# Local attention in 64 by 64 blocks with the band as a product on VectorE, whole turns of q and k, joined tails, token weights in halves, and a new written order

## The chip, the cores and the metric

The kernel runs on one core of a Trainium2 chip. A core has TensorE (PE, with its weight loads listed apart as PEld), VectorE (DVE), ScalarE (ACT), GpSimd (POOL) and SyncE (SP), which here issues all the DMAs. The metric is the device time of one execution in microseconds (us). The kernel before takes 266.62 us in the median of three runs (266.14 to 268.71).

## The reference

The first half is an attention of 8 batches and 8 heads over 576 tokens of 64 channels, made of two parts that are added. The pooled part takes means over 4 tokens, a full softmax attention over the 144 means, and repeats each result 4 times. The local part is a softmax over the keys that lie less than 4 tokens from the query.

```python
q_d = q.reshape(B, H, Sd, 4, D).mean(axis=3)          # and k_d, v_d
out_up = np.repeat(sm_attn(q_d, k_d, v_d), 4, axis=2)
mask = np.abs(pos[:, None] - pos[None, :]) < 4
scores = np.where(mask, scale * q @ k.T, -1e9)
out_local = softmax(scores) @ v
x = (out_up + out_local)                              # batch, 576, 512
```

The second half works on x, token by channel, with a mix over tokens and one over channels:

```python
theta = x @ w_theta
y = w_tok_r @ (x * cos(theta)) + w_tok_i @ (x * sin(theta))
u = x + y
out = u + np.maximum(u @ w_ch, 0.0)
```

Inputs and output are float32; the kernel's products are taken in bfloat16 and summed in float32.

## The kernel before, in words

The work goes batch by batch through generators, one per stage. A string, `ORDER`, has one letter for each step, and each letter runs one step of its stage's generator; `pin` ties every instruction to the one issued before it on its engine, so the string is the order of every engine's queue, SP's too. Several batches are under way at once, and the string was laid out so that steps of different batches stand between each other.

The letters are: L loads (`load`), C casts to bfloat16 (`cast`), A turns of q, k and pooled v (`turns`), S scores (`scores`), N pooled output (`pooled_out`), V local output (`outputs`), T transposes into x (`transposes`), H the product with w_theta with its cosine and sine (`phases`), Z the product of x with these (`modulate`), X the token mix (`mix`), R the channel mix (`channels`), O the last sum and the store (`store`), and l, c, W and D for the weights' loads, casts and turns and for filler matmuls (`warm_up`).

**Turns.** Batches 0 and 1 (`WIDE`) load q and k as 128 partitions of 9 tokens by 64 channels, a run of 2,304 bytes each, and turn them with small matmuls on 64 rows (L299); VectorE sums fours of tokens. Batches 2 to 7 load 96 tokens at a time in runs of 256 bytes, and one matmul with `ip` (L329), an identity with a pooling matrix beside it, gives the turned block and its sums; ScalarE and VectorE copy these out of PSUM in 12 steps (L332, L334 and L336 to L340).

**Local attention.** The queries are cut into 5 chunks of 120, each with 128 keys. For each chunk 8 matmuls (L426, 64 rows and up to 128 columns of weights, two heads beside each other on the two halves of TensorE's rows) write the scores, one exponential on ScalarE empties them (L434), and two selects on GpSimd clear what is outside the band (L447, L449); in batch 0 a product on VectorE does that instead (L440). Then 8 matmuls (L504) make the output and the sum of each row, and VectorE divides (L511, L513).

**Second half.** `mix` makes 8 groups of 9 matmuls a batch (L610) and adds x on VectorE (L614). The last 64 of the 576 tokens, the tail, go a way of their own: in `channels` they take 8 matmuls with 64 columns of weights (L640), and in `mix` and `store` their own copies, DMA transposes (L619) and stores (L662).

**Buffers.** PSUM has two tiles of two banks (`w2`) and four of one bank (`w1`), each used in rotation. Staged loads have 8 buffers, output tiles (`osb`) 4.

Of the kernel before, what the change touches and what calls it, by code (L numbers as in the profile page):

```python
# [15 lines left out]
P = 128  # L16
# [11 lines left out]
QS = [0, 120, 240, 360, 480]  # L28
QC = [120, 120, 120, 120, 96]
KS = [0, 116, 236, 356, 476]  # L30
KW = [128, 128, 128, 128, 100]
QN = [128, 128, 128, 128, 96]
NCH = 5

WIDE = 2
WR = 9
WP = S // WR
TR = 96
TP = TR // 4
TW = TR + TP  # L40

KP = 32

HALF = 64
OC = [128, 128, 128, 128, 64]
# [3 lines left out]
def kernel(  # L49
# [15 lines left out]
    stg = ctx.enter_context(tc.tile_pool(name="stg", bufs=8))  # L65
# [5 lines left out]

    turn2, turn1 = itertools.cycle("ab"), itertools.cycle("abcd")

    def w2(name):
        return ps2.tile([P, 2, 512], FP32, tag="w2" + next(turn2), name=name)
# [3 lines left out]


    staged = {}
    inputs = {}

    def stage(b, key):
        t = staged[b, key] = stg.tile([P, 1024], FP32, tag="st", name=f"st{b}_{key}")
        return t

    def load(b):

        if b < WIDE:  # L90
            for hh in range(4):
                for nm, src in zip("qk", (q, k)):
                    nc.sync.dma_start(
                        out=stage(b, f"{nm}{hh}")[:, 0:WR * D],
                        in_=src[b, 2 * hh:2 * hh + 2].rearrange("h (p r) d -> (h p) (r d)", r=WR),
                    )
                    yield
        else:
            for nm, src in zip("qk", (q, k)):
                for i in range(3):  # L100
                    t = stage(b, f"{nm}{i}")[0:TR].rearrange("p (c h d) -> p c h d", c=2, d=D)
                    for j in range(2):
                        c = 2 * i + j
                        nc.sync.dma_start(
                            out=t[:, j], in_=src[b, :, TR * c:TR * c + TR, :].rearrange("h p d -> p h d"),
                        )
                    yield
        for i in range(3):
            t = stage(b, f"v{i}").rearrange("p (c h d) -> p c h d", c=2, d=D)
            for c in range(2 * i, min(2 * i + 2, NCH)):  # L110
                nc.sync.dma_start(
                    out=t[0:KW[c], c % 2],
                    in_=v[b, :, KS[c]:KS[c] + KW[c], :].rearrange("h p d -> p h d"),
                )
            yield

    def cast(b):

        dims = [P, 2, WR, 2, D] if b < WIDE else [P, 6, H, D]
        q_tm = work.tile(dims, BF16, tag="q_tm", bufs=1, name=f"q_tm{b}")  # L120
        k_tm = work.tile(dims, BF16, tag="k_tm", bufs=1, name=f"k_tm{b}")
        v_w = v_ws[b % 2]
        inputs[b] = (q_tm, k_tm, v_w)
        eng = CASTS.get(b, CASTS[None])
        if b < WIDE:
            for hh in range(4):
                for i, dst in enumerate((q_tm, k_tm)):
                    eng[i](out=dst[:, hh // 2, :, hh % 2, :],
                           in_=staged.pop((b, f"{'qk'[i]}{hh}"))[:, 0:WR * D].rearrange("p (r d) -> p r d", d=D))
                    yield  # L130
        else:
            for i, dst in enumerate((q_tm, k_tm)):
                for c in range(3):
                    eng[i](out=dst[0:TR, 2 * c:2 * c + 2].rearrange("p c h d -> p (c h d)"),  # L134
                           in_=staged.pop((b, f"{'qk'[i]}{c}"))[0:TR])
                    yield
# [148 lines left out]
    def turns(b):  # L285
# [75 lines left out]
        for s in range(2):  # L361
# [5 lines left out]
            )  # L367
        yield

    pds, pms, xds, tmps = {}, {}, {}, {}  # L370

    def slot(b, h):

# [363 lines left out]
```

## Time and profile before

| | before |
|---|---|
| runs, median (lowest to highest) | 266.62 us (266.14 to 268.71) |
| profiled execution, first to last instruction | 266.2 us |
| PE busy | 239.5 us, 90% |
| VectorE busy | 180.8 us, 68% |
| ScalarE busy | 165.9 us, 62% |
| GpSimd busy | 167.9 us, 63% |
| DMA queue, share of 16 engines | 84.2% |
| DMA packets under 512 bytes | 121,777 of 131,155 |
| ScalarE table loads | 18 of 1,283 ns |

The span of the profiled execution lies 0.4 us under the median of the runs; the profile gives no other time of that execution. Busy time of TensorE is modelled from overlapping matmuls, so the rate of a form is better read from the distance between the starts of rows in the timeline than from the mean duration.

### The profile page before, as it was taken

To read this page: it belongs to the slowest core of one execution; us is meant where nothing else is said; L and a number is where in the kernel's file an instruction comes from. 1 tells how busy PE (TensorE), PEld (TensorE's weight loads), DVE (VectorE), ACT (ScalarE), POOL (GpSimd) and SP (SyncE) were. 2 spreads that over 40 slices of the span, in tenths; PEclk is the share of its full clock that TensorE was granted. 3 is DMA by queue.
4 is the path that set the end of the run, shared out by engine and by line. 5 is a ranking of instruction groups with operands and counts; after the bars stand their busy time and mean duration, and the time that the engine had idled before them with its cause. 6 is when DMAs were issued, how large, how long until landed. Compare 5 with 4: busy or idle time off the path is not lost. (4 is left out here: it accounts for less than half of the span.)

```text
span 266.2 us, 7362 instructions
## 1 busy us (share of the span) xinstructions
PE 239.5 (90%) x2880; PEld 164.6 (62%) x2880; DVE 180.8 (68%) x406; ACT 165.9 (62%) x312; POOL 167.9 (63%) x223
## 2 busy tenths in 40 slices
PE   2467898989988999899999999989999999999990
PEld 1234555778655777577676778756658666777740
DVE  3566998867495656875695767756877658855443
ACT  3663289663997699836987787547865699350000
POOL 4459746997989757686939467968765892400000
PEclk9999999999999999999999999999999999999997
DMA  7998999998989995599857998998779942304446
GB/s 230 314 284 283 317 224 188 208 201 168 222 139 213 236 198 115 117 196 284 176 110 144 243 258 147 111 216 207 184 154 210 270 88 64 102 21 105 105 149 215
DMA packets 131155, 49.34 MB, mean 185 GB/s; under 512 B 121777, under 2 KB 122801, under 8 KB 131121
## 3 DMA queue, kind: packets, MB, share of 16 engines
q1 hardware_dynamic: 131120, 48.88, 84.2%
q8 instruction: 22, 0.36, 0.6%
q14 instruction: 13, 0.10, 0.2%
HBM read 33.65 MB, written 9.44 MB: 162 GB/s over the span
## 5 line engine op out<-in xcount | busy, mean ns | idle before, releaser
L610 PE MATMUL psu<-WT,z 128*128 128x288 bf16 x576 | 79.5, 286 | 0.0
L610 PEld LDWEIGHTS <-z 128*128 128x128 bf16 x576 | 53.8, 98 | 14.7 <-issue 0.4
L434 ACT ACTIVATE pm<-psS 128x1024 bf16<-128x1024 f32 (+1 forms) x40 | 38.6, 989 | 16.7 <-PE psS L426 15.5
L614 DVE TENSOR_TENSOR uT<-psu,xT 128x288 bf16<-128x288 f32 x64 | 28.9, 454 | 28.2 <-PE psu L610 28.0
L447 POOL TENSOR_SCALAR_AFFINE_SELECT pm<-pm 128x1024 bf16<-128x1024 bf16 (+1 forms) x35 | 36.7, 1049 | 14.1 <-ACT pm L434 14.1
L449 POOL TENSOR_SCALAR_AFFINE_SELECT pm<-pm 128x1024 bf16<-128x1024 bf16 (+1 forms) x35 | 36.8, 1051 | 2.4
L553 PE MATMUL psth<-wth,xT 128*128 128x512 bf16 x128 | 32.4, 379 | 0.6 <-DVE xT L535 0.4
L632 PE MATMUL psr<-wch,uT 128*128 128x512 bf16 x128 | 31.4, 379 | 0.6 <-DVE xT L535 0.6
L140 POOL CAST v_w<-st_v 128x1024 bf16<-128x1024 f32 (+1 forms) x24 | 21.9, 916 | 15.2 <-DMA st_v<-in_v_dram 15.2
L332 ACT CAST kT<-pstr 128x384 bf16<-128x384 f32 x36 | 17.6, 489 | 19.0 <-PE pstr L329 18.8
L513 DVE TENSOR_TENSOR tmp<-psloc,rl 120x512 bf16<-120x512 f32 (+1 forms) x40 | 27.6, 690 | 1.4
L558 ACT ACTIVATE cs<-psth,pihc 128x512 bf16<-128x512 f32 x32 | 22.2, 693 | 9.1 <-PE psth L553 5.3
L535 DVE TENSOR_TENSOR xT<-xTps,xdT 128x480 bf16<-128x480 bf16 (+1 forms) x40 | 24.9, 631 | 3.7 <-PE xTps L534 3.6
L654 DVE SCALAR_TENSOR_TENSOR osb<-psr,ur 128x512 f32<-128x512 f32 x32 | 21.5, 684 | 6.4 <-PE psr L632 4.3
L617 POOL COPY ut<-uT 128x64 bf16<-128x64 bf16 x32 | 7.3, 237 | 27.7 <-DVE uT L614 22.6
L134 POOL CAST k_tm<-st_k 96x1024 bf16<-96x1024 f32 x18 | 18.9, 1051 | 7.8 <-DMA st_k<-in_k_dram 5.5
L134 POOL CAST q_tm<-st_q 96x1024 bf16<-96x1024 f32 x18 | 18.8, 1048 | 7.6 <-DMA st_q<-in_q_dram 7.6
L588 DVE TENSOR_TENSOR z<-psxt,cs 128x1024 bf16<-128x1024 bf16 x32 | 21.5, 682 | 3.1 <-PE psxt L587 3.0
L332 ACT CAST qT<-pstr 128x384 bf16<-128x384 f32 x36 | 16.9, 484 | 8.6 <-PE pstr L329 8.5
L334 DVE CAST qdT<-pstr 128x96 bf16<-128x96 f32 x36 | 9.1, 255 | 17.4 <-ACT qT L332 16.9
L559 ACT ACTIVATE cs<-psth 128x512 bf16<-128x512 f32 x32 | 19.2, 600 | 0.0
L632 PEld LDWEIGHTS <-uT 128*128 128x128 bf16 x128 | 11.5, 97 | 11.7 <-DVE xT L535 0.6
(97 smaller groups left out, 419.0 us busy)
## 6 DMA issues: line engine op xcount, KB each, us to landing
st_v<-in_v_dram SPq DMA_DIRECT2D x32, 256.0 KB, 5.0
out_dram<-osb SPq DMA_DIRECT2D x32, 256.0 KB, 3.2
st_q<-in_q_dram SPq DMA_DIRECT2D x36, 192.0 KB, 4.9
st_k<-in_k_dram SPq DMA_DIRECT2D x36, 192.0 KB, 4.1
st_q<-in_q_dram SPq DMA_DIRECT2D x8, 288.0 KB, 4.9
st_k<-in_k_dram SPq DMA_DIRECT2D x8, 288.0 KB, 5.4
st_v<-in_v_dram SPq DMA_DIRECT2D x8, 200.0 KB
stw_tok<-in_moe_w_tok_r_dram SPq DMA_DIRECT2D x4, 288.0 KB
```

The lines of the kernel that those rows point to most:

```text
L134: eng[i](out=dst[0:TR, 2 * c:2 * c + 2].rearrange("p c h d -> p (c h d)"), in_=staged.pop((b, f"{'qk'[i]}{c}"))[0:TR])
L332: nc.scalar.copy(out=To[:, :, TR * c:TR * c + TR], in_=ps[:, :, 0:TR])
L434: nc.scalar.activation(out=pv, in_=ps[0:kw].rearrange("p e (j w) -> p (e j) w", w=P)[:, :, 0:qn], func=AF.Exp, scale=SCL,)
L447: nc.gpsimd.affine_select(out=pv, in_=pv, compare_op=ALU.is_ge, fill=0.0, base=off, pattern=[[0, 8], [-1, qn]], channel_multiplier=1)
L449: nc.gpsimd.affine_select(out=pv, in_=pv, compare_op=ALU.is_ge, fill=0.0, base=6 - off, pattern=[[0, 8], [1, qn]], channel_multiplier=-1)
L513: nc.vector.tensor_tensor(out=tmp[0:cnt].rearrange("p (e j d) -> p e j d", e=2, j=4), in0=pv[0:cnt, :, :, 0:D], in1=rl[0:cnt].unsqueeze(3) ...
L535: nc.vector.tensor_tensor(out=xT[:, :, QS[c]:QS[c] + cnt].rearrange("p e (m j) -> p e m j", j=4), in0=ps[:, :, 0:cnt].rearrange("p e (m j) ...
L553: nc.tensor.matmul(out=th, lhsT=xT[:, dc, P * c:P * c + P], rhs=wth[:, dc, :], start=(dc == 0), stop=(dc == 3),)
L558: nc.scalar.activation(out=cs[:, 0, :], in_=th, func=AF.Sin, bias=pihc, scale=1.0)
L610: nc.tensor.matmul(out=ps[:, 0:288], lhsT=z[:, j, P * dc:P * dc + P], rhs=WT[:, j, cols], start=(j == 0), stop=(j == 8),)
L614: nc.vector.tensor_tensor(out=uT[:, dc, cols], in0=ps[:, 0:288], in1=xT[:, dc, cols], op=ALU.add)
L632: nc.tensor.matmul(out=psr, lhsT=uT[:, dc, P * c:P * c + P], rhs=wch[:, dc, :], start=(dc == 0), stop=(dc == 3),)
```

## The change

All batches now load q and k as 2,304-byte runs, turn them with 9 full transposes of 128 by 128 to a group of four heads (`turns`, 4 steps a batch, each emptied by one ScalarE copy of 1,152 elements), and take the sums of four apart (`sums`): those of k on VectorE, those of q on GpSimd with two additions, but in batch 0 on VectorE. The tokens are cut into 10 blocks of 58, each with a window of 64; queries and keys have the same window. Two blocks make a chunk and lie on the two halves of the partitions, so score and output matmuls work on 64 rows by 64 columns of TensorE's array, four tiles beside each other. Two chunks share one exponential. The band is a product on VectorE in all batches (`masks`). The tails of two batches are joined to 128 rows for their transposes, channel mix and store. Token weights come in two halves of their output tokens, and batch 0 mixes the first half first. Residual transposes, the last sums and the stores are steps of their own. Staged loads have 15 smaller buffers, output tiles 5, and there are 4 filler steps in place of 5, all at the end. `ORDER` is new, with 814 letters for 658.

```diff
...
-WIDE = 2
...
+W = 64
+STEP = 58
+CH = 2 * STEP
+W0 = [min(max(STEP * n - 3, 0), S - W) for n in range(10)]
+OWN = [min(STEP, S - STEP * n) for n in range(10)]
+UNITS = [(0, 1), (2, 3), (4,)]
...
-    stg = ctx.enter_context(tc.tile_pool(name="stg", bufs=8))
+    stg = ctx.enter_context(tc.tile_pool(name="stg", bufs=15))
...
     def load(b):
+        for hh in range(4):
+            for nm, src in (("k", k), ("q", q)):
+                nc.sync.dma_start(out=stage(b, f"{nm}{hh}"),
+                                  in_=src[b, 2 * hh:2 * hh + 2].rearrange("h (p r) d -> (h p) (r d)", r=WR))
+                yield
+        for c in range(NCH):
+            t = stage(b, f"v{c}")[:, 0:DM].rearrange("p (h d) -> p h d", d=D)
+            for g in range(2):
+                lo = W0[2 * c + g]
+                nc.sync.dma_start(out=t[W * g:W * g + W], in_=v[b, :, lo:lo + W, :].rearrange("h p d -> p h d"))
+            yield
...
-    CASTS = {0: (act, gp, gp), None: (gp, gp, gp)}
+    CASTS = {0: (act, dve, gp), None: (gp, gp, gp)}
...
     def turns(b):
+        for i in range(2):
+            for n, (tm, To) in enumerate(((k_tm, kT), (q_tm, qT))):
+                ps = w2(f"pstr{n}{i}_{b}", BF16).rearrange("p k e -> p (k e)")
+                for r in range(WR):
+                    nc.tensor.transpose(out=ps[:, P * r:P * r + P], in_=tm[:, i, r, :, :], identity=ident)
+                EVAC[n](
+                    out=To[:, 2 * i:2 * i + 2, 0:S].rearrange("p a (w r) -> p a w r", r=WR),
+                    in_=ps[:, 0:P * WR].rearrange("p (r a w) -> p a w r", a=2, w=W),
                 )
+                yield
...
+    EVAC = (act, act)
...
+    def sums(b):
+        for i in range(2):
...
+                nc.vector.tensor_reduce(out=kd[:, hs, :, 0:PG].rearrange("p e g m -> p (e g) m"), axis=AX.X, op=ALU.add,
+                                      in_=kT[:, hs, :].rearrange("p e (g m j) -> p (e g) m j", m=PG, j=4))
+                yield
+                if i < QSUM.get(b, QSUM[None]):
+                    nc.vector.tensor_reduce(out=qdT[:, hs, :], axis=AX.X, op=ALU.add,
+                                            in_=qT[:, hs, :].rearrange("p e (m j) -> p e m j", j=4))
                 else:
...
+                    nc.gpsimd.tensor_tensor(out=two, in0=four[:, :, 0:2], in1=four[:, :, 2:4], op=ALU.add)
+                    nc.gpsimd.tensor_tensor(out=qdT[:, hs, :].rearrange("p e m -> p (e m)"),
+                                            in0=two[:, :, 0], in1=two[:, :, 1], op=ALU.add)
+                yield
...
+    QSUM = {0: 2, None: 0}
...
+    def scores(b):
+        for u, cs in enumerate(UNITS):
...
+            ps = w2(f"psS{u}_{b}")
+            for i, c in enumerate(cs):
+                for hh in range(4):
+                    for g in range(2):
+                        lo = W0[2 * c + g]
+                        for e in range(2):
+                            nc.tensor.matmul(
+                                out=ps[W * g:W * g + W, e, 4 * W * i + W * hh:4 * W * i + W * hh + W],
+                                lhsT=kT[64 * e:64 * e + 64, hh, lo:lo + W],
+                                rhs=qT[64 * e:64 * e + 64, hh, lo:lo + W],
+                                start=True, stop=True,
+                            )
+            pm = pms[b, u] = work.tile([P, 2, n, 4, W], BF16, tag=f"pm{n}", bufs=3, name=f"pm{u}_{b}")
+            nc.scalar.activation(out=pm.rearrange("p e c j w -> p e (c j w)"), in_=ps[:, :, 0:4 * W * n],
+                                 func=AF.Exp, scale=SCL)
+            yield
...
+    def masks(b):
+        for u, cs in enumerate(UNITS):
...
+            MASK.tensor_tensor(out=pv, in0=pv, in1=band.unsqueeze(1).to_broadcast([P, n, W]), op=ALU.mult)
+            yield
...
+    MASK = nc.vector
...
     def outputs(b):
+        for u, cs in enumerate(UNITS):
+            for i, c in enumerate(cs):
...
+                for j in range(4):
+                    for hf in range(2):
...
+                        for g in range(2):
+                            nc.tensor.matmul(
+                                out=pv[W * hf:W * hf + W, g, j, :],
+                                lhsT=pms[b, u][W * g:W * g + W, e, i, blk, :],
+                                rhs=v_w[W * g:W * g + W, c, 4 * hf + j, 0:65],
+                                start=(j == 0), stop=(j == 3),
+                            )
...
     def transposes(b):
...
+            for g in range(2):
...
+                for kk in range(2):
+                    nc.tensor.matmul(
+                        out=ps[:, kk::2, STEP * g:STEP * g + OWN[n]],
+                        lhsT=tmp[:, g, P * kk:P * kk + P], rhs=identw[:, :, lo:lo + OWN[n]],
+                        start=True, stop=True,
+                    )
...
+    def tail_channels(i):
+        ut = uts[i]
+        psr = rels["t", i] = w1(f"psrt_{i}")
+        for dc in range(4):
+            nc.tensor.matmul(out=psr, lhsT=ut[:, dc, :, :], rhs=wch[:, dc, :], start=(dc == 0), stop=(dc == 3))
+        yield
...
-            osb = moep.tile([P, DM], FP32, tag="osb", bufs=4, name=f"osb{c}_{b}")
+            osb = osbs[b, c] = moep.tile([P, DM], FP32, tag="osb", bufs=5, name=f"osb{c}_{b}")
...
-    WARM = 5
+    WARM = 4
...
+        P=each(pooled_scores), S=each(scores), M=each(masks), N=each(pooled_out), n=each(pooled_turn),
+        V=each(outputs), T=each(transposes), H=each(phases), h=each(tail_z), Z=each(modulate),
+        X=each(mix), r=each(residual), t=each(tail_residual, 4), R=each(channels), Q=each(tail_channels, 4),
+        O=each(relu), q=each(tail_relu, 4), o=each(store), s=each(tail_store, 4),
```

Of the new letters, a is `sums`, U and u make the pooled v, P the pooled scores, M the masks, n the turn of the pooled output, w the turns of the weights, h the tail's product and its DMA transpose, r the residual transposes; t, Q, q and s are the joined tails'.

## The prediction

> **What bounds the kernel now.** I read the busy time by stretch first, to see which engine leaves no room. Its columns are the stretch, its length, busy us (and instructions) of PE, PEld, DVE, ACT and POOL, the granted clock, the DMA share and GB/s.
>
> ```profile
> 0.00:27.00 27.00, 14.87 (x166) 8.06 (x166) 14.91 (x50) 13.57 (x19) 16.29 (x36) 1.00 0.95 277
> 40.00:120.00 80.00, 75.99 (x978) 54.26 (x979) 56.63 (x129) 59.57 (x120) 65.08 (x75) 1.00 0.97 183
> 120.00:240.00 120.00, 117.80 (x1429) 83.03 (x1427) 85.09 (x184) 85.08 (x162) 77.64 (x96) 1.00 0.80 165
> 253.00:266.20 13.20, 6.38 (x40) 2.79 (x38) 5.36 (x9) 0.00 (x0) 0.24 (x1) 0.88 0.56 181
> ```
>
> From 40 us to 253 us TensorE is covered 95 to 100%, while the other three stand at about 70%. Time is lost at the start (half empty to 27 us) and in the last 13 us. So an edit is worth what it takes from TensorE's own queue in the middle, and what it takes from the chains at both ends. What TensorE really spends is read next in the timeline, from start to start, because the durations overlap.
>
> ```profile
> 37.88 0.44 PE L299 MATMUL pstr<-ident,q_tm 64*128 64x64 bf16 x18
> 50.67 0.44 PE L466 MATMUL psnd<-vd,pd 128*72 128x65 bf16 x8
> 66.12 0.30 PE L408 MATMUL psSd<-qdT,kdP 64*32 64x144 bf16 x8
> 105.63 0.42 PE L504 MATMUL psloc<-v_w,pm 128*128 128x65 bf16 x8
> 105.98 0.40 PE L426 MATMUL psS<-qT,kT 64*128 64x128 bf16 x8
> 106.31 0.43 PE L489 MATMUL psxd<-ident,xd 72*128 72x72 bf16 x8
> ```
>
> The reader is to subtract the last instruction's own duration (its form's mean) from a row and divide by the gaps. L504: 0.42 less 0.197 is 0.223 over 7 gaps, 32 ns for each matmul. L426: 0.40 less 0.216 is 0.184 over the 3 gaps between 4 pairs, 61 ns for a pair: two heads on the two halves of the rows run beside each other. L299: 0.44 less 0.212 over the 8 gaps of 9 pairs, 28 ns for a pair of 64 columns. L408: 0.30 less 0.238 leaves 62 ns from the first four to the second four, each four on tiles of their own, with 144 columns moving. And L489 starts 0.33 after L426, that is 0.146 after its last pair where 0.061 would do: changing the tiling of the array costs about 0.09 us.
>
> Last, the groups that the change touches on the other engines (the last line is from the view of one source line, with minimum, median and maximum ns):
>
> ```profile
> L434 ACT ACTIVATE pm<-psS 128x1024 bf16<-128x1024 f32 (+1 forms) x40 | 38.6, 989 | 16.7 <-PE psS L426 15.5
> L447 POOL TENSOR_SCALAR_AFFINE_SELECT pm<-pm 128x1024 bf16<-128x1024 bf16 (+1 forms) x35 | 36.7, 1049 | 14.1 <-ACT pm L434 14.1
> L449 POOL TENSOR_SCALAR_AFFINE_SELECT pm<-pm 128x1024 bf16<-128x1024 bf16 (+1 forms) x35 | 36.8, 1051 | 2.4
> L440 DVE TENSOR_TENSOR pm<-pm,band x5: 548/949/1226, 19.0 to 32.7; 128x1024 bf16<-128x1024 bf16 x4, 100x768 bf16<-100x768 bf16 x1
> ```
>
> These are large, but they belong to engines that are not the bound.
>
> **The change part by part, on TensorE.** *Local products.* Before: 160 pairs at 0.061 and 320 output matmuls at 0.032, 9.8 + 10.2 = 20.0 us. After: 640 score and 640 output matmuls of 64 by 64, in 320 fours on four tiles. No row shows a four with 64-column weights. Bounds: as fast as the pair of 64 columns, 28 ns, 9.0 us in all; two pairs in turn, 56 ns, 17.9 us; all four in turn at 32 ns, 128 ns, 41.0 us. I take 35 ns: L408 shows four tiles beside each other, and L466, with 72 columns of weights, steps at 34 ns ((0.44 - 0.204) / 7), so narrow weights set a pace near that. 320 x 0.035 = 11.2, **-8.8 us** (-11.0 to -2.1; +21.0 if in turn).
>
> The Trainium skill speaks against this: "TensorE: Matmul & The Clock Gate", the section "Wait — 56ns, not 53.3ns?", says that starts never come closer than about 25 ns however small the matmul. By it 640 + 640 matmuls could not take under 32 us, and this part would cost 12 us. The 18 starts of L299 in 0.23 us are 13 ns apart, so for matmuls on different tiles the row is not bound by that rule, and the row decides.
>
> *Tiling changes.* I counted them in both strings, a step's letter giving its shape: 132 before, 105 after, since most score steps and output steps, now of the same shape, stand beside each other, and since the tails and the turns of batches 0 and 1 no longer use small tiles. 27 x 0.09 = **-2.4 us** (0 to -2.4).
>
> *Turns.* Batches 2 to 7 had 288 matmuls at 52 ns from start to start (four in 0.21 us), batch 1 had 36 pairs at 28: 16.0 us. Batches 1 to 7 now have 252 transposes at 57 (the 128 by 128 transposes of L587, four in 0.39 with 0.22 for the last): 14.4. **-1.6 us** (-2 to 0).
>
> *Tails.* 32 pairs at 0.106 (L640) were 3.4 us; 16 matmuls of 512 columns at 0.216 are 3.5. Nothing, their tiling changes are counted. *Mix, phases, channels and transposes to x* keep their columns within 4%: nothing.
>
> *Fillers.* Of the five groups of six at 0.216, three (28.4, 36.3 and 67.8 us) lay past the start, 3.9 us; all now stand at the end, behind the last real product. They may have filled gaps: **-2 us** (-3.9 to 0).
>
> **Off TensorE.** ScalarE: 16 exponentials at 1.03 and 8 near 0.65 for 38.6, and 32 copies near 1.13 (0.645 for 576 elements, 0.83 ns for each more) for 53.8: about 166 to 131 us. GpSimd: 73.5 us of selects go, 14 pairs of additions come (0.61 for 256 elements gives 1.38 + 0.69, 29 us; at the selects' 1 ns an element 12), small casts and copies even out: about 168 to 120. DMA: 55,296 runs of 256 bytes become 6,144 of 2,304. None of these was the bound, so I give nothing but the cover: the queues wait less.
>
> VectorE gets more. Masks: 16 at 0.95 and 8 at 0.55, 19.6 for 4.5, +15.1 (+9 with the 0.69 of the first one, +20 with 1.23). Sums of k: 16 of 1,160 elements at 1.36 (the row of 1,152 has 1.35) and 2 for q, 24.5, for 20.7 of sums and of the pooled q's copies. Casts of batch 0's q, near 0.67 each, and 18 half copies of weights against 9, less 3.0 of turns copied: +1. In sum 181 to 201 us. A mask stands in VectorE's queue ahead of the divisions that free PSUM for TensorE, and of the sums of x that the phases wait for. Now 6.0 us of TensorE's waits end on VectorE (the filler's first wait aside). Busy over idle grows from 181/85 = 2.1 to 201/52 = 3.9; by that ratio the waits become 11. **+5 us** (0 to +12).
>
> The page "SBUF — State Buffer" of the skill, section "Who interferes with whom", says that a VectorE instruction with two inputs from SBUF blocks, or is blocked by, a GpSimd instruction that reads it, for the whole instruction. L440 fits: 0.69 us alone, up to 1.23 beside casts. By the rule every mask could also wait out one cast (about 1 us), 24 us at most; with GpSimd busy under half the time that would be 11, which lies inside what I took.
>
> **Both ends.** Start: in batch 0 the exponentials on ScalarE go from 4.9 to 2.7 us, the turns' copies from 3.9 to 4.5, and v is loaded ahead of the weights; but no filler warms the array, which still ran at half rate at 23 us (six filler matmuls in 2.74 us, 1.46 later). **-2 us** (-6 to +4). End:
>
> ```profile
> 258.75 0.63 PE L640 MATMUL psr<-wch,uT 128*64 128x256 bf16 x8
> 259.74 2.18 DVE L654 SCALAR_TENSOR_TENSOR osb<-psr,ur 128x512 f32<-128x512 f32 x3 [1.56 <-DMA out_dram<-osb]
> 262.17 0.42 DVE L654 SCALAR_TENSOR_TENSOR osb<-psr,utr 128x256 f32<-128x256 f32 x1 [0.25 <-DMA out_dram<-osb]
> ```
>
> TensorE ends at 259.4, the span 6.8 later, because four output buffers wait for their stores. With five, and the joined tail ahead of the last rows, one sum (0.68), one issue (0.53) and a store (about 3.2) follow: 4.4. **-2.5 us** (-4 to 0).
>
> **Sum.** -8.8 - 2.4 - 1.6 - 2 + 5 - 2 - 2.5 = -14.3; 266.2 less that is 251.9, and the runs' median lies 0.4 above that span: 252.3. By the small unknowns of opposite signs this case reaches from 243 to 260.
>
> **Rivals.** *VectorE takes the bound.* For: 201 us of work, at least 12 idle at the start and 8 at the end, and 28 us in which it waits for the mix's products anyway make 249; the masks at 1.23 add 5. Against: before, it idled 85 us and little of that hurt TensorE. With half of its remaining idle time (37 us) kept it ends near 266, 258 to 275.
>
> *Loads set the pace of the first half.* The DMA share is 0.95 or more to 120 us, and 18 us of GpSimd's casts wait for it. If TensorE gains nothing up to there, two fifths of the middle's 14.8 us are lost: 258. Against: q and k now come in long runs.
>
> *Slower: the four tiles do not run beside each other.* Then the local products take 41.0 and not 11.2 us: 282. It decides from (20.0 + 5.5) / 320 = 80 ns a four on, 5.5 being the other terms' gain. L408 speaks against it; for it, that no row has 64 by 64 tiles following each other without a pause.
>
> **Chances.** Forecast 0.58, loads 0.12, VectorE 0.23, tiles in turn 0.07. Of VectorE's case I count 0.06 faster, 0.07 within 1% (which is about what runs between 266.1 and 268.7 can tell from no change) and 0.10 slower. So faster 0.76, same 0.07, slower 0.17. The range from 243 to 270 leaves out the lowest of the forecast (0.05), the top of VectorE's case and the tiles in turn (0.13).
>
> **What would show it.** In the profile after: score and output rows whose fours start about 35 ns apart; ScalarE near 131, GpSimd near 120 and VectorE near 201 us; TensorE still covered 95% from 40 us on, and under 5 us from its last real product to the end. I am wrong if TensorE's waits behind VectorE or behind the two-bank PSUM tiles grow by more than 12 us, or if fours start 80 ns apart.

## The result and the profile after

In four runs each on one chip the changed kernel takes 259.26 us (257.11 to 261.75) and the kernel before 267.28 (266.14 to 268.71): a ratio of **0.965, 95% interval 0.957 to 0.973**. (Ratios leave out executions more than 1.5% above the fastest of the same kernel, here 261.75, so they are not the quotient of the medians.) The forecast was 252.3 in a range from 243 to 270. So the direction and the range hold, and a little over half of the forecast gain is there. The profiled execution of the changed kernel spans 258.0 us, 8.2 less than the 266.2 of before; the sum had said 14.3 less.

The busy time by stretch of the changed kernel, with the columns as before, and the page's row of the granted clock in 40 slices:

```profile
0.00:27.00 27.00, 11.00 (x192) 7.91 (x192) 17.00 (x58) 12.27 (x15) 14.59 (x47) 1.00 0.94 278
40.00:120.00 80.00, 74.74 (x1222) 52.68 (x1220) 60.74 (x124) 48.62 (x67) 53.75 (x80) 0.94 0.93 227
120.00:232.00 112.00, 108.18 (x1645) 75.21 (x1634) 94.24 (x183) 69.53 (x99) 36.77 (x55) 1.00 0.64 144
```

```profile
PEclk9999999589999999979999999999999999999999
```

TensorE is still covered 93% (second row) and 97% (third) of the time. VectorE has come closer to it, from 71 to 76% in the second row and from 71 to 84% in the third. But the covered time of the second row is no longer all at full speed: its clock is 0.94, and the row of the clock shows where, in the eighth slice (5) and in the eighteenth (7). Before, every slice but the last read 9.

The row reads 9 at the start too, but there it has no record of the clock yet and counts that as full. The timeline shows what the array really did, first of the changed kernel, then of the kernel before:

```profile
27.28 1.12 PE L267 MATMUL pstr<-ident,k_tm 128*128 128x128 bf16 x9 [0.74 <-DVE rl L454]
...
32.51 0.67 PE L267 MATMUL pstr<-ident,q_tm 128*128 128x128 bf16 x9
```

```profile
22.99 2.74 PE L275 MATMUL wu<-warm,ident 128*128 128x512 bf16 x6
...
28.38 1.46 PE L275 MATMUL wu<-warm,ident 128*128 128x512 bf16 x6
```

Nine transposes of one shape take 1.12 us and then 0.67, six fillers 2.74 and then 1.46. The first record says full clock from 32.5 us in the changed kernel and from 27.5 in the kernel before. So the array stayed at half rate 5 us longer than before.

The rows that answer to those of before, from the timeline, start to start:

```profile
118.61 0.30 PE L356 MATMUL psSd<-qdT,kd 64*32 64x144 bf16 x8
...
122.05 0.46 PE L375 MATMUL psS<-qT,kT 64*64 64x64 bf16 x32
122.33 0.30 PE L447 MATMUL psloc<-v_w,pm 64*64 64x65 bf16 x16
...
132.25 0.68 PE L267 MATMUL pstr<-ident,q_tm 128*128 128x128 bf16 x9
```

L375: 0.46 less its mean of 0.201 leaves 0.259 for 31 gaps, 8.4 ns each, 33 ns for four tiles. L447: 0.30 less 0.202 over 15 gaps is 6.5 ns, 26 ns for four, but this is one of the quickest of its rows: from 53 us on and outside half clock, the starts of both forms together lie 8.4 ns apart, 34 ns for four. And L447 starts 0.28 after L375, so nothing is paid between these two steps of one shape. L267: 0.68 less 0.236 over 8 gaps is 55 ns for a whole transpose. The forecast had 35 for both fours and 57.

The groups that the change touches, kept apart by shape:

```profile
L268 ACT COPY qT<-pstr 128x1152 bf16<-128x1152 bf16 x16 | 18.1, 1133 | 7.0 <-PE pstr L267 7.0
L268 ACT COPY kT<-pstr 128x1152 bf16<-128x1152 bf16 x16 | 18.0, 1126 | 16.3 <-PE pstr L267 16.1
L382 ACT ACTIVATE pm<-psS 128x1024 bf16<-128x1024 f32 x16 | 16.2, 1024 | 9.9 <-PE psS L375 9.9
L290 POOL TENSOR_TENSOR two<-qT 128x576 f32<-128x576 bf16 x14 | 16.0, 1146 | 7.9 <-ACT qT L268 7.9
...
L390 DVE TENSOR_TENSOR pm<-pm,band 128x1024 bf16<-128x1024 bf16 x16 | 12.9, 809 | 0.3 <-ACT pm L382 0.3
```

The prices off TensorE came out near their estimates (1.13 us a copy; 0.81 a mask where 0.95 was taken; 1.15 for the first addition where 1.38 was).

### Where the 8.2 us come from

To split TensorE's time I gave every form its steady distance from start to start, read as above, and counted what lies beyond it: at a change of the array's tiling up to 0.1 us as that change, the rest as a pause, and everything beyond it in a half-clock stretch as half clock. The distances are mine, so a row is good to perhaps 1 us. From 27.5 us, where before's clock is full, to the start of the last real product:

| us of TensorE's time | before | after | change | forecast |
|---|---|---|---|---|
| columns (products, transposes) | 195.9 | 184.6 | -11.3 | -10.4 |
| fillers | 3.9 | 0 | -3.9 | -2 |
| tiling changes | 9.9 | 7.3 | -2.6 | -2.4 |
| pauses and small delays | 21.7 | 26.6 | +4.9 | +5 |
| half clock | 0 | 5.5 | +5.5 | 0 |
| **27.5 us to the last real product's start** | **231.4** | **224.0** | **-7.4** | -9.8 |
| last real product's end to the end | 6.8 | 6.0 | -0.8 | -2.5 |

The half-clock row holds the two stretches of the clock's row alone. By the same count the 5 us from 27.5 to 32.5 hold 2.6 us more of half clock; 2.1 of it stand above among the pauses, the rest among the tiling changes. So half clock takes about 8 us, and the pauses grew by about 3.

The work went as forecast. Half clock, for which the sum has no term past the start, is the largest row that the forecast lacks; the start (forecast -2) does not show as less work left after 27.5 us; the end gives a third of its term.

### The profile page after: what moved, and what is told of

Its sections match the earlier page's. It is cut to its first block, busy times and chain, and to the rows that moved or that the text cites. A ratio compares the mean times of both kernels' runs of the same rounds, so it can differ in the third digit from the quotient of the medians.

```text
span 258.0 us, 8100 instructions
## 1 busy us (share of the span) xinstructions
PE 229.7 (89%) x3332; PEld 157.8 (61%) x3332; DVE 196.5 (76%) x404; ACT 138.9 (54%) x190; POOL 118.0 (46%) x201
## 4 chain that ended last, share of the span: by engine, by line
PE 63%; DVE 12%; DMA 8%; ACT 6%; POOL 6%; issue 4%; SPq 0%; DVEq 0%; POOLq 0%; ACTq 0%
PE psu L558 25%; PE psr L588 7%; PE psth L501 6%; PE pstr L267 6%; DMA z<-zT 4%; PE xTps L480 3%; DVE tmp L456 2%; DMA st_k<-in_k_dram 2%; DVE xT L485 2%; PE wu L160 2%; PE psS L375 2%; PE psxt L537 2%; POOL full_pu L96 2%; PE psnd L403 2%; PE psloc L447 2%
## 5 line engine op out<-in xcount | busy, mean ns | idle before, releaser
L198 POOL CAST v_w<-st_v 128x512 bf16<-128x512 f32 x40 | 26.1, 664 | 30.3 <-DMA st_v<-in_v_dram 16.1
L456 DVE TENSOR_TENSOR tmp<-psloc,rl 128x512 bf16<-128x512 f32 x40 | 27.7, 692 | 1.4
L382 ACT ACTIVATE pm<-psS 128x1024 bf16<-128x1024 f32 (+1 forms) x24 | 20.5, 883 | 14.9 <-PE psS L375 14.7
L268 ACT COPY kT<-pstr 128x1152 bf16<-128x1152 bf16 x16 | 18.0, 1126 | 16.3 <-PE pstr L267 16.1
L538 DVE TENSOR_TENSOR z<-psxt,cs 128x1024 bf16<-128x1024 bf16 x32 | 21.5, 684 | 6.2 <-PE psxt L537 3.8
L485 DVE TENSOR_TENSOR xT<-xTps,xdT 128x464 bf16<-128x464 f32 (+1 forms) x40 | 24.7, 629 | 1.0 <-PE xTps L480 0.4
L607 DVE SCALAR_TENSOR_TENSOR osb<-psr,ur 128x512 f32<-128x512 f32 x32 | 21.5, 685 | 5.0 <-DMA ur<-uT 3.5
L194 POOL CAST k_tm<-st_k 128x576 bf16<-128x576 f32 x28 | 19.4, 694 | 5.5 <-DMA st_k<-in_k_dram 5.2
L268 ACT COPY qT<-pstr 128x1152 bf16<-128x1152 bf16 x16 | 18.1, 1133 | 7.0 <-PE pstr L267 7.0
L281 DVE TENSOR_REDUCE kd<-kT 128x290 bf16<-128x1160 bf16 x16 | 21.6, 1353 | 0.0
L194 POOL CAST q_tm<-st_q 128x576 bf16<-128x576 f32 x28 | 18.7, 667 | 5.0 <-DMA st_q<-in_q_dram 4.9
L390 DVE TENSOR_TENSOR pm<-pm,band 128x1024 bf16<-128x1024 bf16 (+1 forms) x24 | 18.9, 787 | 1.0 <-ACT pm L382 1.0
L267 PE MATMUL pstr<-ident,k_tm 128*128 128x128 bf16 x144 | 12.1, 236 | 8.4 <-ACT k_tm L194 7.1
```

The lines of the kernel that those rows point to most:

```text
L194: eng[i](out=dst[:, hh // 2, :, hh % 2, :], in_=staged.pop((b, f"{nm}{hh}")).rearrange("p (r d) -> p r d", d=D))
L198: eng[2](out=v_w[:, c, :, 0:D], in_=staged.pop((b, f"v{c}"))[:, 0:DM].rearrange("p (h d) -> p h d", d=D))
L267: nc.tensor.transpose(out=ps[:, P * r:P * r + P], in_=tm[:, i, r, :, :], identity=ident)
L268: EVAC[n](out=To[:, 2 * i:2 * i + 2, 0:S].rearrange("p a (w r) -> p a w r", r=WR), in_=ps[:, 0:P * WR].rearrange("p (r a w) -> p a w r", a ...
L281: nc.vector.tensor_reduce(out=kd[:, hs, :, 0:PG].rearrange("p e g m -> p (e g) m"), axis=AX.X, op=ALU.add, in_=kT[:, hs, :].rearrange("p e ...
L456: nc.vector.tensor_tensor(out=tmp.rearrange("p g (j d) -> p g j d", d=D), in0=pv[:, :, :, 0:D], in1=rl.unsqueeze(3).to_broadcast([P, 2, 4, ...
```

## The experiments

Times are medians over all runs of a kernel, with the lowest and highest, and ratios are to the kernel before, run beside it. Milestones in us from the profiles' timelines: the first score product, the first mix group of batches 0, 1 and 7, the last mix group, the end of the last real product, the span, and the half-clock stretches from 27.5 us to the last real product. "To 32.5" means half rate from before 27.5 us to there.

| kernel | first score | mix 0 | mix 1 | mix 7 | last mix | last product | span | half clock |
|---|---|---|---|---|---|---|---|---|
| before | 17.2 | 51.2 | 83.9 | 242.3 | 251.7 | 259.4 | 266.2 | none |
| before, without its fillers | 17.2 | 53.5 | 85.9 | 244.7 | 254.1 | 261.8 | 268.1 | 45.5-48.9 |
| after | 17.6 | 50.4 | 78.7 | 234.4 | 243.0 | 252.0 | 258.0 | to 32.5, 46.1-53.0, 111.0-114.4 |
| after, again | 17.6 | 49.0 | 77.8 | 234.0 | 242.6 | 251.0 | 257.1 | to 33.7, 108.8-112.2 |
| fillers at weight turns | 17.6 | 51.0 | 80.5 | 236.8 | 245.3 | 254.2 | 259.8 | to 31.5, 113.5-116.9 |
| modulate before store | 17.5 | 48.8 | 78.7 | 236.3 | 244.9 | 253.4 | 259.5 | to 31.5 |
| tail late | 17.5 | 48.8 | 80.5 | 236.4 | 245.0 | 253.1 | 259.2 | to 31.1, 58.4-61.8, 96.0-99.4 |
| set-up on GpSimd | 13.2 | 45.4 | 74.0 | 232.1 | 240.6 | 249.4 | 255.5 | to 29.4, 135.2-138.7 |
| the same, again | 13.2 | 46.7 | 75.4 | 232.2 | 240.7 | 249.8 | 255.9 | to 28.6, 42.3-49.1 |
| set-up and tail | 13.0 | 44.8 | 73.1 | 230.1 | 238.7 | 246.9 | 252.9 | to 29.1, 104.2-111.1 |
| set-up and a third of the masks | 13.1 | 45.7 | 75.1 | 230.9 | 239.5 | 248.4 | 254.5 | to 31.2, 106.3-109.7 |
| no band product | 17.6 | 46.4 | 74.8 | 232.0 | 240.6 | 249.0 | 255.1 | to 30.3, 108.8-112.2 |
| four of one tile in a row | 17.6 | 50.0 | 79.4 | 235.4 | 244.0 | 252.1 | 258.2 | to 32.4, 46.0-52.9 |
| scores twice | 17.6 | 50.1 | 81.5 | 243.3 | 251.9 | 260.4 | 266.5 | to 32.2, 114.1-117.6 |

### Does the half clock cost the missing time?

My first theory: the lost us are the half-clock stretches, so executions with a higher mean clock are shorter. The rival: the clock falls where TensorE would have waited anyway. First the changed kernel again, unedited:

> The changed kernel again, unaltered, beside the runs of the next three. Theory: its time moves with the granted clock of the execution (257.1 us at 1.0 and 259.7 us at 0.98 so far), so between 257 and 262 us, and the executions with the higher mean clock are the shorter ones. Rival: the clock has no part in it, and times and clocks are unrelated.

Measured: 260.06 us (258.68 to 262.86), ratio 0.972 [0.967, 0.977]. The two shortest executions, 258.68 and 258.84, and the longest, 262.86, all have a mean clock of 0.993; those at 0.967 and 0.973 lie between them. Past the start, its profile has 3.4 us at half clock where the first had 10.3, and ends 0.9 us sooner. So the mean clock does not rank the executions. But that mean counts the time before the first record as full clock, 32.5 us of it in the first profile and 33.7 in this one, though the array ran at half rate; so this doesn't decide between the theory and the rival.

The stretches themselves, in the profile of the changed kernel (columns as before):

```profile
42.00:46.00 4.00, 3.76 (x112) 2.78 (x110) 3.76 (x10) 3.97 (x7) 3.92 (x7) 1.00 0.38 136
46.10:53.00 6.90, 6.90 (x92) 4.26 (x92) 5.13 (x14) 3.19 (x6) 3.32 (x6) 0.51 0.78 244
111.00:114.40 3.40, 3.40 (x23) 2.44 (x21) 2.81 (x6) 0.00 (x0) 1.34 (x2) 0.50 1.04 293
```

```profile
42.13 0.72 PE L375 MATMUL psS<-qT,kT 64*64 64x64 bf16 x64
42.79 1.77 PE L245 MATMUL wps<-ident,wtm 128*128 128x128 bf16 x18
44.49 0.40 PE L537 MATMUL psxt<-ident,xT 128*128 128x128 bf16 x4
44.72 0.91 PE L245 MATMUL wps<-ident,wtm 128*128 128x128 bf16 x6
45.75 0.32 PE L375 MATMUL psS<-qT,kT 64*64 64x64 bf16 x16
```

Ahead of the first stretch TensorE is busy 3.76 of 4.0 us, but with transposes and 64 by 64 products alone; the half clock follows. The second follows a real pause, 2.41 us at 109.63 (below). The repeated run has the same products in the same order there, and keeps full clock:

```profile
42.00:46.00 4.00, 3.76 (x112) 2.80 (x111) 3.83 (x10) 3.97 (x7) 3.92 (x8) 1.00 0.40 146
45.00:53.00 8.00, 7.72 (x141) 5.75 (x141) 7.86 (x22) 4.11 (x7) 4.62 (x8) 1.00 0.70 200
```

So these products alone don't decide it; what else does is open. The Trainium skill, "TensorE: Matmul & The Clock Gate", "Part 4: PE-mode transpose", says that transposes do not count as busy for the clock in the way that other products do; the rows of the first profile agree with it. No run here takes the transposes alone.

Fillers put back at the place of the weights' turns, and none behind the last product:

```diff
-    WARM = 4
+    WARM = 2
...
-        "aHHlAlwLLLZTCaAccwcwwwLcHHLwSSacwLCLwwhcwLwlZaLCCLCCwwMCSwCLZwPMPwUwLuVVCLXNCCLNXLALnCATCXMCLLCaLALL"
+        "aHHlAlwLLLZTCaAccwcwwwLcHHLwSSacwDLCLwwhcwLwlZaLCCLCCwwMCSwDCLZwPMPwUwLuVVCLXNCCLNXLALnCATCXMCLLCaLA"
...
```

> Two of the four fillers at the end are moved between the turns of the token weights (after the 8th and the 15th of 18 steps), the other two are dropped. Theory (the clock is halved at 46 us, because for some us before only transposes and small tiles run): the 6.8 us at half clock there go, 3.4 us are won and 2.6 us of fillers paid, so the time falls by 0 to 2 us, and the mean clock rises from 0.98 to about 0.99. Rival (the fillers are only work): the half clock stays and the time grows by 2 to 3 us. The dropped fillers at the end are worth at most 0.4 us by either, since the last store lands 0.4 us before the last filler ends.

Measured: 260.94 us (257.91 to 262.25), ratio 0.972 [0.966, 0.978], no gain on the repeated run's 0.972. Its profile has half clock at the start to 31.5 and at 113.5, and none near 46 us; but neither has the repeated run's, without fillers there.

Then the pause at 109.63. A last sum (`osb`, L607) stands ahead of the modulate product (`z`, L538) in VectorE's queue, and waits for a DMA transpose:

```profile
108.29 0.69 DVE L607 SCALAR_TENSOR_TENSOR osb<-psr,ur 128x512 f32<-128x512 f32 x1 [3.51 <-DMA ur<-uT]
...
108.89 0.68 DVE L538 TENSOR_TENSOR z<-psxt,cs 128x1024 bf16<-128x1024 bf16 x1
...
109.63 0.54 PE L558 MATMUL psu<-WT,z 128*128 128x288 bf16 x3 [2.41 <-DVE z L538]
```

```diff
-        "CVCSLaTMCLXXUaCSLSCTLLLXVVLLMLHrArTCCLCHXuAAaZoTHCAXCLaLHLrLZZHhrLPLPtMRRLCCLRLOOZOCCSVoXXNCaLaCXCCC"
+        "CVCSLaTMCLXXUaCSLSCTLLLXVVLLMLHrArTCCLCHXuAAaZoTHCAXCLaLHLrLZZHhrLPLPtMRRLCCLRLOZOOCCSVoXXNCaLaCXCCC"
```

> One step of the order is moved: the last product of x with cosine and sine of batch 2 stands ahead of the first last-sum of batch 1, which waits 3.5 us on VectorE for a residual transpose, where TensorE waits 2.4 us for that product and the clock is halved right after. Theory: the 2.4 us of waiting and the 3.4 us at half clock (1.7 us lost) at 107 to 114 us both go, so 2 to 4 us less. Rival: the wait moves to the next product or to a transfer, and the time stays within 1 us.

Measured: 260.0 us (258.34 to 261.2), ratio 0.972 [0.967, 0.977]: nothing won, though its profile has no half clock at all after 31.5 us. That speaks for the rival: with both later stretches gone, their 5.5 us do not come back, as far as one profile of each kernel can show. What takes their place is spread over many pauses and isn't shown to have one cause.

The other direction, the kernel before without its fillers at 28.4, 36.3 and 67.8 us (three letters D less in its `ORDER`):

```diff
-    WARM = 5
+    WARM = 2
...
```

> The kernel before without the three fillers at 28, 36 and 68 us. The prediction's term: they cost up to 3.9 us of TensorE, so 0 to 4 us faster, 2 taken. Rival (they keep the clock up): stretches at half clock appear between 28 and 110 us, the mean clock falls below 0.99, and the time stays the same or grows by up to 4 us.

Measured: 269.14 us (267.6 to 273.32), ratio 1.006 [1.002, 1.011]. Taking 3.9 us of filler work away makes it about 1.6 us slower, and its profile has half clock from 45.5 to 48.9, where before's has none. It starts its first mix group 2.3 us later and keeps about that distance to the end. So in the kernel before those fillers were no cost, and my -2 for their going has the wrong sign there. That they helped through the clock is not shown.

### Is TensorE's pace the bound, and do four tiles run beside each other?

The order inside a step was changed so that four matmuls of one tile follow each other, in scores and outputs:

```diff
...
-                for hh in range(4):
-                    for g in range(2):
-                        lo = W0[2 * c + g]
-                        for e in range(2):
+                for g in range(2):
+                    for e in range(2):
+                        lo = W0[2 * c + g]
+                        for hh in range(4):
...
-                for j in range(4):
-                    for hf in range(2):
-                        blk, e = slot(4 * hf + j)
-                        for g in range(2):
+                for hf in range(2):
+                    for g in range(2):
+                        for j in range(4):
+                            blk, e = slot(4 * hf + j)
```

> The same score and output matmuls, but with the loops exchanged so that four matmuls in a row have the same tile of the array, in place of four different ones. Theory (four tiles run beside each other, about 29 ns a four): now each costs about 30 ns alone, a four 90 to 120, and 320 fours cost 20 to 29 us more, most of it in the time. Rival (TensorE does not need the neighbours to be on different tiles, or is not the bound): less than 8 us more.

Measured: 263.66 us (259.93 to 264.37), ratio 0.977 [0.966, 0.988], between 1 and 3 us over the kernel after by the ratios (0.965 and 0.972), with intervals that overlap. In the timeline:

```profile
107.45 0.48 PE L375 MATMUL psS<-qT,kT 64*64 64x64 bf16 x31
107.74 0.19 PE L447 MATMUL psloc<-v_w,pm 64*64 64x65 bf16 x1
107.76 0.19 PE L375 MATMUL psS<-qT,kT 64*64 64x64 bf16 x1
...
119.73 0.35 PE L447 MATMUL psloc<-v_w,pm 64*64 64x65 bf16 x16
```

Less the means of 0.203 and 0.202, L447 steps at 9.8 ns and L375 at 9.3. These are quick rows; over all of them past 53 us the starts lie 10.9 ns apart, for 8.4 in rotation: 44 ns for four, and 3.2 us more for all 1,280 products. Nothing like the slow rival's 80 ns appears; rotation helps by about a quarter. But this is not the price of four products in turn on one tile. The second and third rows show a first output product that starts ahead of the last score product, which stands before it in the queue: products of different tiles pass each other, so the edit did not keep one tile busy alone.

Then each score product twice, with the same result:

```diff
-                        for e in range(2):
+                        for e in (0, 1, 0, 1):
```

> The kernel after with each of its 640 score matmuls issued twice with the same result: 160 more fours on four tiles, TensorE's work alone grows. If TensorE is the bound and a four takes 29 ns in the middle, it is 4.6 us slower than the kernel after (about 264 to 265 us beside 260). If a four costs the 56 ns of two pairs in turn, 9 us. If VectorE or the loads set the pace, 0 to 2 us.

Measured: 272.74 us (268.15 to 273.12); the profiled execution is the shortest, a span of 266.5, 8.5 over the first profile of the kernel after and 9.4 over the second; the other three are 4 to 5 us longer.

```profile
126.49 0.74 PE L375 MATMUL psS<-qT,kT 64*64 64x64 bf16 x64
...
177.42 0.28 PE L375 MATMUL psS<-qT,kT 64*64 64x64 bf16 x10 [3.38 <-issue]
```

64 products take 0.74 where 32 took 0.46: 0.28 for 8 fours, 35 ns each, 5.6 us for all 160 (0.28 for each of sixteen pairs of chunks, half of it for each of eight single ones). The pause of 3.38 us in the middle of a score step is one of several for which the profile names no releaser (`issue`). The waits from 27 us on, and the instruction queue's line of the page, here and in the kernel after:

```profile
PE psS L375 <- issue: 5.3, 4, 3.4
...
PE psth L501 <- issue: 1.8, 1, 1.8
```

```profile
q8 instruction: 31, 0.51, 0.9%
```

```profile
q8 instruction: 26, 0.43, 0.7%
```

That is 7.1 us in five waits; the kernel after has one such wait of 0.6 us. The queue q8 brings instructions in packets of 16 KB: 31 for the 3,972 matmuls here and as many weight loads, 26 for 3,332, one for about 256 instructions. By the packets' own times in the trace, each of these five waits, and the one of the kernel after, ends 1.2 to 1.5 us after such a packet has ended; the packet before the longest runs from 174.1 to 175.9, and TensorE goes on at 177.42. So TensorE seems to have waited for its own instructions, though no run varies that. Counted as in the table of the 8.2 us, the 8.5 us are 5.6 of work, about 6 of pauses, and about 4 less of half clock. So the time is near that of two pairs in turn but the mechanism is not. The added work did not go into waits that were there already, which fits an engine at the bound; a clean price of the work it is not.

### What does VectorE's new work cost?

The band product left out. This leaves out part of the computation: keys outside the band are counted in the local softmax.

```diff
...
-            n = 8 * len(cs)
-            pv = pms[b, u].rearrange("p e c j w -> p (e c j) w")
-            MASK.tensor_tensor(out=pv, in0=pv, in1=band.unsqueeze(1).to_broadcast([P, n, W]), op=ALU.mult)
             yield
```

> The changed kernel without the products with the band, so that each local softmax runs over its whole window of 64 keys: the work left out is 24 instructions and 18.9 us of VectorE. The prediction's term (VectorE's load costs TensorE about 5 us in waits): 4 to 6 us faster. Rival (VectorE has room, the gaps come from DMA waits and order): within 2 us.

Measured: 257.14 us (255.67 to 260.9), ratio 0.959 [0.953, 0.965], 2 to 3 us under the kernel after's two medians, for 24 masks that are 18.9 us of VectorE's time. The milestones say where: mix 0 begins at 46.4 and not at 49.0 to 50.4, but from there to the last real product it takes 202.6 us, where the two profiles of the kernel after took 201.6 and 202.0. So what the masks cost lies at the start, and nothing shows in the middle. Part of it may be the clock, which is full from 30.3 us here and from 32.5 and 33.7 there.

### The start

VectorE's first work is to build constant matrices, in turns with GpSimd. Here is the kernel after:

```profile
11.42 0.17 DVE L99 COPY pu<-full_pu 64x32 bf16<-64x32 bf16 x1 [1.16 <-POOL full_pu L96]
...
12.73 2.73 DVE L194 CAST q_tm<-st_q 128x576 bf16<-128x576 f32 x4
...
14.20 1.14 PE L267 MATMUL pstr<-ident,q_tm 128*128 128x128 bf16 x9 [5.98 <-DVE q_tm L194]
```

The four casts of batch 0's q, which I had priced at 0.67 us each, stand behind that building until 12.73, and TensorE's turns of q wait 5.98 us. The edit puts the whole building on GpSimd:

```diff
-        nc.vector.memset(full, val)
+        nc.gpsimd.memset(full, val)
...
-            nc.vector.tensor_copy(out=t[W * g:W * g + W, :], in_=full[W * g:W * g + W, g, 0:n])
+            nc.gpsimd.tensor_copy(out=t[W * g:W * g + W, :], in_=full[W * g:W * g + W, g, 0:n])
```

> The pooling matrices and the band are filled and copied on GpSimd in place of VectorE, so that VectorE's four casts of batch 0's q no longer stand behind twelve microseconds of turns between the two engines. Theory: the casts run from about 4 to 11 us as q lands, the first scores come at about 13.5 and not at 17.6 us, and the end comes 1 to 4 us sooner. Rival: the first mix is held by the weights' loads and turns, it still starts at 50 us, and the time stays within 1 us.

Measured: 257.25 us (254.39 to 258.63), ratio 0.958 [0.949, 0.966], beside 0.972 [0.967, 0.977] for the kernel after. Its timeline:

```profile
4.46 0.75 DVE L194 CAST q_tm<-st_q 128x576 bf16<-128x576 f32 x1 [0.60 <-DMA st_q<-in_q_dram]
...
13.18 0.33 PE L375 MATMUL psS<-qT,kT 64*64 64x64 bf16 x8 [0.17 <-ACT kT L268]
```

The first cast now follows its load, at 4.46, the first score comes 4.4 us sooner, and 2.4 of that is left at the last mix group. The same once more, beside the variants below:

> The kernel after with the start's matrices built on GpSimd alone, once more, so that the two variants of it stand beside it on one chip. 257 to 258 us, ratio 0.955 to 0.965 of before, if the earlier gain of about 1.5% was its own; near 0.972, as the kernel after had, if it was chance.

Measured: 255.94 us (254.64 to 257.77), ratio 0.954 [0.948, 0.960]. Both rounds lie below the kernel after (0.958 and 0.954, beside 0.965 and 0.972), so the gain is the edit's own, at 1 to 2%.

With it, the third of each three band products moved to GpSimd, batches 1 to 7:

```diff
-            MASK.tensor_tensor(out=pv, in0=pv, in1=band.unsqueeze(1).to_broadcast([P, n, W]), op=ALU.mult)
+            (nc.gpsimd if u == 2 and b else MASK).tensor_tensor(out=pv, in0=pv, in1=band.unsqueeze(1).to_broadcast([P, n, W]), op=ALU.mult)
```

> The kernel after, with the start's matrices on GpSimd, and the third of each three band products (batches 1 to 7, 512 elements) on GpSimd in place of VectorE. VectorE loses 7 products of 0.74 us, 5.2 us of its about 196, of some 19 for all products; GpSimd gains 7 of about 1.1 us (2.0 ns an element by its additions). If VectorE's queue costs about 3 us for all products, as leaving them out suggested, a quarter of that comes back: 0.5 to 1 us under the run with the start alone. If a product on GpSimd waits behind the casts and blocks VectorE while it runs, it is the same or up to 2 us slower.

Measured: 257.26 us (254.75 to 260.44), ratio 0.957 [0.950, 0.964]. VectorE's busy time falls from 193.1 to 190.6 us, and no time is won. The 0.5 to 1 us in question is smaller than these intervals, so this is a weak second sign that VectorE does not set the pace in the middle.

### The end

The last rows of the kernel after, and the last two pieces of the chain that ended last:

```profile
250.19 0.69 DVE L613 SCALAR_TENSOR_TENSOR osbt<-psrt,utr 128x512 f32<-128x512 f32 x1 [2.62 <-DMA utr<-ut]
250.80 2.54 DVE L607 SCALAR_TENSOR_TENSOR osb<-psr,ur 128x512 f32<-128x512 f32 x4
...
250.93 1.02 PE L588 MATMUL psr<-wch,uT 128*128 128x512 bf16 x4 [0.64 <-DVE osbt L613]
...
251.79 5.34 PE L160 MATMUL wu<-warm,ident 128*128 128x512 bf16 x24
252.13 2.02 SPq L619 DMA_DIRECT2D out_dram<-osb  x4
```

```profile
247.64 2.43 DMA utr<-ut
251.96 5.18 PE wu L160 x24
```

Two things are late. VectorE waits 2.62 us for the joined tail's DMA transpose while four sums of batch 7 stand behind it. And 24 fillers behind the last real product run to 257.1, past the last store (252.13 + 2.02, and about 2.5 to land): the chain ends in the fillers. They cost little, though. The run with fillers at the weights' turns has none behind its last product, which ends at 254.2, and still needs 5.6 us to the end at 259.8, where this one needs 6.0:

```profile
253.09 2.54 DVE L607 SCALAR_TENSOR_TENSOR osb<-psr,ur 128x512 f32<-128x512 f32 x4
...
254.43 2.03 SPq L619 DMA_DIRECT2D out_dram<-osb  x4
```

There the last of four sums ends 1.4 us after the last product, the last store is issued at 256.04 and has landed 3.0 us later, and 0.85 us more pass to the end of the span.

The next edit puts batch 7's rows ahead of the joined tail:

```diff
-        "hOrOUVoSaQRqMZrPPuXOoNtsXNXnTTVVXToHQTqXHZXTHZHXHsRhOZoZXrRrrrrOROoXoXXrXoXrROXroXXRrrtOROROQRRRqOoo"
-        "ORoDsOoDoODoDo"
+        "hOrOUVoSaQRqMZrPPuXOoNtsXNXnTTVVXToHQTqXHZXTHZHXHsRhOZoZXrRrrrrOROoXoXXrXoXrROXroXXRrrtORORORRROooOR"
+        "oQOoOooqoDsDDD"
```

> The joined tail of the last two batches is taken after the last rows of batch 7, on TensorE, VectorE and SyncE, in place of ahead of them. Theory: VectorE no longer waits 2.6 us for the tail's DMA transpose with the last rows' sums behind it, and TensorE not 0.6 us; the end comes 1 to 2 us sooner. Rival: the last residual transpose holds the end anyway and the time stays within 0.5 us.

Measured: 260.06 us (256.91 to 262.15), ratio 0.967 [0.961, 0.973]: it can't be told from the kernel after's 0.972 [0.967, 0.977]. Together with the set-up on GpSimd:

> The kernel after, with the start's matrices built on GpSimd and batch 7's rows finished ahead of the last joined tail. If the tail's DMA transpose in front of the last rows is what kept the end at 15 us, this is 0.5 to 2 us under the run with the start alone (ratio near 0.950 of before). If the end is set by the chain from the last channel mix to its store whatever stands first, it equals that run within 0.4%.

Measured: **254.5 us (253.68 to 257.22), ratio 0.949 [0.943, 0.955]**, the shortest of all, ahead of both kernels. From its last mix group to the end it takes 14.2 us, the kernel after 15.0 and the set-up alone 15.2. That is not yet a gain of the tail: with the old end the repeated kernel after takes 14.5 and the one with four of one tile in a row 14.2, and the intervals of 0.949 and 0.954 overlap. Its fillers begin at 246.69 and last 5.34 us, to 252.03; the tail's last store is issued at 249.0 and, by the 2.4 us that such stores take in the median, lands near 251.4. So here the fillers hold the end, by about 0.6 us; no run takes them from this version.

## Why the prediction was right, and where it was not

- **TensorE is the bound:** right as far as shown. TensorE is covered 93 to 97% from 40 us on, added score work did not go into its waits, and what was taken from VectorE in the middle bought nothing. No run adds or removes TensorE work alone without changing pauses or clock.
- **Local products -8.8:** right in mechanism, and nearly in size. At 34 ns, 320 fours are 10.8 us for the 11.2 I took, so -9.2. The row that I set against the 25 ns rule decided rightly: starts are 8.4 ns apart on average. The rival of tiles in turn (282 us) is out: no row has fours 80 ns apart, and with four of one tile in a row in the queue the time grows by a few us at most.
- **Turns -1.6 and tiling changes -2.4:** the transposes step at 55 ns for 57 taken, and the reckoning above gives -2.6 for the changes (about -3 with the start's half clock taken out). No run takes either alone.
- **Fillers -2:** wrong sign, as far as the kernel before shows it: without them it is 1.6 us slower, not 2 faster. Their 3.9 us of work went, but I gave "they may have filled gaps" an upper bound of 0, and no price to what else they may do, for the clock for instance.
- **Not in the sum: the clock.** I read 1.00 in before's rows and took it as given, though the change takes away the fillers and puts transposes and small products next to each other. The sum speaks of half rate at 23 us, but has nothing past the start. 5.5 us of the new profile lie in the two later stretches, and 2.6 more between 27.5 and 32.5, where the kernel before was at full rate. That this is the missing gain is not shown: the mean clock can't rank the runs, since it leaves out the start, and without the later stretches the time stayed.
- **VectorE's waits +5:** the number looks right by luck. Pauses grew by 4.9 in all, of which 2.1 are the half rate to 32.5 us. TensorE's waits that end on VectorE grew from 6.0 to 13.2, and 6.0 of that is the one wait for batch 0's q at 14.2, not for masks. Leaving the masks out wins 2 to 3 us, at the start. The ratio of busy to idle time spread the price evenly; what was found of it stands at the start.
- **Start -2:** the profile gives -0.8 at the first mix group, within the bounds, with the array at half rate 5 us longer than before. I counted the casts of q at 0.67 each on VectorE and didn't look at what stands ahead of them in its queue. That was worth 4.4 us at the first score and 2 to 4 in the medians.
- **End -2.5:** got -0.8; the last real product is 6.0 us from the end, not under 5. I wrote myself that the fillers stand behind the last real product. 24 at 0.216 are 5.2 us, longer than the 4.4 I gave the whole end, and the chain ends in them. But without them 5.6 us remain. The 4.4 had one sum of 0.68 behind the last product, where the sums end 1.4 after it; 0.4 more go to the last store's issue, and the 0.85 us from its landing to the end of the span were left out.
- **The median 0.4 above the span:** a wrong step. In every execution with both, device time is 1.7 us over the span (268.0 and 266.3 for the kernel before, 259.73 and 258.0 after). The span of 266.2 belonged to one of the longer executions and not to the median.
- **Off TensorE:** GpSimd 118.0 us (120 forecast) and VectorE 196.5 (201). ScalarE is at 138.9 and not 131: its exponentials fell from 38.6 to 21.0 and its turn copies from 53.8 to 36.1, together the 35 expected, but the page's busy time is less than the sum of its groups.
- **Rivals:** VectorE as the bound would have given 266; the runs without masks and with fewer of them speak against it, the second weakly. Loads as the pace of the first half gave 258, near the measured time, yet the mix groups of batch 1 begin 5.2 us sooner than before, at 78.7, so the first half did gain.

## What to carry to other kernels

Before pricing an operation that is moved to an engine's start, list what already stands in that queue ahead of it: here a few tiny copies, each waiting for another engine, cost more than all the casts behind them. Where a change removes filler work or bunches transposes, put the clock into the sum as a term with two ends. And check each term against the plain length of what you yourself say stands there: the fillers at the end were longer than the whole term, and more sums stood there than the one it priced.

## What the runs showed of the hardware that I had not expected

Products of 64 by 64 start 8.4 ns apart on average on four tiles in rotation, and 10.9 ns apart when the queue has four in a row for one tile; there, products of one tile started ahead of earlier ones of another. The clock fell to half for 6.9 us after 4 us in which TensorE was busy 94% of the time with transposes and small products alone, and in a second execution of the same kernel, with the same 4 us, it did not. The page's row of the clock reads full before the first record, while the array ran at half rate to 32.5 us. And with 640 products more, TensorE stood still up to 3.38 us at a time with no releaser in the profile, each time until 1.2 to 1.5 us after the end of a 16 KB packet of its instruction queue; that this is the cause is not tested.
